# A gate made of pairs of nested tanh, with the first feed-forward tile reordered

## The chip, the cores and the metric

The kernel runs on one core of one Trainium2 chip. The core has five engines that each follow a list of their own: PE (TensorE, matmuls; PEld is its weight load), DVE (VectorE), ACT (ScalarE), POOL (GpSimd) and SP (SyncE, which here issues most DMAs). The metric is the device time of one execution in microseconds, as a median over runs; the profile is of one execution.

## The reference, cut to what matters

```python
# 4 x 8 heads of 768 x 64: attention in which only equal hash buckets see each other
x = attn_out.transpose(0, 2, 1, 3).reshape(3072, 512)
h = x @ w_in                                   # 3072 x 2048
sp = np.maximum(h, 0.0) + np.log1p(np.exp(-np.abs(h)))
g = h * erf(sp)                                # the gate
return (g @ w_out).astype(np.float32)          # 3072 x 512
```

## The kernel before

**Two parts.** Attention over 16 pairs of heads runs first, up to about 312 us. Then the feed-forward part takes the 3072 tokens in six tiles of 512 (t = 0 to 5). Both matrix products are done with seven block products in place of eight (Strassen in Winograd's form), so there are block sums around them, on DVE and POOL.

**Tile 0.** Its first product is done by one level: seven products P1 to P7 (`plain`), each in four chunks c = 0 to 3, 28 steps in all. A step accumulates into a PSUM bank named M1, M2, M4, M5, M6 or M7; `read_plain` copies a bank to one of four quarters of `h` on ACT, `complete` adds a bank to a quarter on DVE. A bank is free for the next step when it has been read. Chunks 0 and 1 make the first half (fl = 0) of each quarter, chunks 2 and 3 the second.

**Tiles 1 to 5.** Each of the seven products is done by seven smaller ones (`small`, Q1 to Q7). Their weight sums (`presum_inner`, called "inner") are made once by POOL while tile 0 runs, staged in a room, and written to DRAM by `keep_inner`, SP's transfers to `wi_P1` to `wi_P7`; `load_wi` brings them back into a ring that overlays `w_in`. POOL also makes the operand sums, `presum_x` (L347) and `presum_xi` (L1481).

**The gate.** Each quarter's half is a unit of 128 x 1024 numbers; six tiles have 48. `h * erf(softplus(h))` is computed as h times tanh of a product of factors. On ACT: `lead` (L1626, a sigmoid), `factor` (L1630, three sigmoids with scale and bias) and `saturate` (L1647, tanh). On DVE: `multiply` (L1636, one for each factor) and `gate` (L1651). Tiles `e` and `w` have two rooms each, so two units are in work at a time.

**The second product.** `presum_g` (L1696) sums gated quarters, `project` (L1725) multiplies them with `w_out` in seven products M1 to M7, interleaved on PE with the next tile's small products; `combine` (L1759 on DVE) adds and the result goes out. `presum_w` (L1443) makes the block sums of `w_out` on DVE: eight of them, into `wt`.

**The last pair of heads.** Its normalisation runs beside tile 0 (`late`): PE sums a divisor (`X`), ACT copies it, SP sends it through DRAM to be spread (`zd`, `zc`), DVE inverts it (L760, L763), SP spreads the inverse (`rd`, then `r`, which lands in `area`), DVE multiplies it in (`x_last`, L789), and SP writes the result. `late` 3 to 6 on DVE (L815) are the second halves of the weight sums P5, P6, P7 and P3. Tile 1's load of x waits for this chain.

**What sets the order.** Every operation is entered with an engine, a cost and a rank; `arrange` simulates the engines with these costs and picks, for each engine, the open operation that starts first, ties by rank. The result is a fixed list for each engine, which the hardware follows in order. Costs and ranks thus change only order.

Of the kernel before, what the change touches and what calls it, by code (L numbers as in the profile page):

```python
# [73 lines left out]
GATE_LEAD = float(np.exp(0.024672653620378578))  # L74
GATE_BIAS = 0.2070990400060388
GATE_S = tuple(
    (a, b, float(np.exp(d)))
    for a, b, d in (
        (1.0042202890675247, -2.7392697200635756, -1.6980318627393862),
        (0.9963684715182539, -0.22837759957137604, 0.7457328010609228),  # L80
        (1.6743181256578874, -5.977511012430903, 0.8413097454356667),
    )
# [106 lines left out]
def kernel(  # L189
# [45 lines left out]
    cq = const.tile([P, len(GATE_S) + 1], F32, name="cq")  # L235
# [56 lines left out]
    for j, c in enumerate([b for _, b, _ in GATE_S] + [GATE_BIAS]):  # L292
        nc.vector.memset(cq[:, j : j + 1], c)
# [936 lines left out]
    def feed_forward(pools, check, late):  # L1230
# [109 lines left out]
        def plain_ops():  # L1340
            for c in range(4):
                x, y, z = (("M1", "M2", "M4"), ("M5", "M6", "M7"))[c % 2]
                for k, (name, where, q, fn) in enumerate(
                    (
                        ("P1", x, 0, read_plain),
                        ("P2", y, 0, complete),
                        ("P6", x, 1, read_plain),
                        ("P5", z, 3, read_plain),
                        ("P7", x, 3, complete),
                        ("P3", z, 1, complete),  # L1350
                        ("P4", x, 2, read_plain),
                    )
                ):
                    fl = c // 2
                    pe(
                        "P",
                        (name, c),
                        1.73,
                        (0, (c + k / 7) / 4),
                        plain,  # L1360
                        (c, name, where, name in ("P1", "P2", "P5"), name in ("P4", "P2", "P3")),
                        reads=(xkey(0, name), ("w", name, fl)),
                        writes=(("bank", where),),
                    )
                    op(
                        (fn.__name__, c, q),
                        "ACT" if fn is read_plain else "DVE",
                        0.58 if fn is read_plain else 0.69,
                        (0, (c + k / 7) / 4),
                        fn,  # L1370
                        (c, q, where),
                        reads=(("bank", where),),
                        writes=part(0, q, fl),
                    )


        stage = [kept[f"h{n}"][:, :, :, :].rearrange("p l c t -> p (l c t)").rearrange("p (n c) -> p n c", n=4) for n in (4, 5)]

        def presum_inner(name, n, k):

            a = w_of(name)
            a11, a12 = a[:, 0, 0:WP], a[:, 1, 0:WP]
            a21, a22 = a[:, 0, WP:FH], a[:, 1, WP:FH]
            s1, s2, s3, s4 = (stage[n % 2][:, m, :] for m in range(4))
# [6 lines left out]
            nc.gpsimd.tensor_tensor(out=out_, in0=one_, in1=two_, op=op_)  # L1391

        def keep_inner(name, n):
            nc.sync.dma_start(out=wi_dram[name][:, 3:7, :], in_=stage[n % 2])
            if name in ("P6", "P7", "P5", "P3"):
                a = w_of(name)
                nc.sync.dma_start(out=wi_dram[name][:, 0:2, :], in_=a[:, 0:2, 0:WP])
                nc.sync.dma_start(out=wi_dram[name][:, 2, :], in_=a[:, 1, WP:FH])

        def inner_ops():  # L1400
            for n, name in enumerate(CHAIN):
                both = (("w", name, 0), ("w", name, 1))
                rooms = tuple(("h", 4 + n % 2, fl, tl) for fl in range(2) for tl in range(2))
                for k in range(4):
# [40 lines left out]
        def presum_w_ops():  # L1445
            for k in range(4):
                for fl in range(2):
# [3 lines left out]
                        1.25,  # L1451
                        (2, 0.2 + k / 10, fl),
                        presum_w,
                        (fl, k),
                        writes=(("wt", (3, 1, 2, 0)[k], fl),),
# [90 lines left out]
        def chain_ops(t):  # L1546
            for i, name in enumerate(CHAIN):
# [6 lines left out]
                    2.0,  # L1554
                    (1, t + (i - 1.2) / 7, 1),
# [67 lines left out]
        def lead(t, q, fl):  # L1623
            s = st["s", t, q, fl] = own("e")
            n = len(GATE_S)
            nc.scalar.activation(out=s, in_=unit(t, q, fl), func=AF.Sigmoid, bias=cq[:, n : n + 1])  # L1626

        def factor(t, q, fl, j):
            f = st["q", t, q, fl, j] = own("w")
            nc.scalar.activation(  # L1630
                out=f, in_=unit(t, q, fl), func=AF.Sigmoid, scale=GATE_S[j][0], bias=cq[:, j : j + 1]
            )

        def multiply(t, q, fl, j):
# [4 lines left out]
                scalar=GATE_S[j][2],  # L1639
# [12 lines left out]

        READY = {0: 3 / 7, 2: 5 / 7, 3: 6.3 / 7, 1: 1.0}

        def gate_ops(t, q):
            for fl in range(2):
                me = (t, q, fl)
                when = t + (READY[q] if t or again else (0.55, 1.0)[fl] + 0.03 * (0, 3, 1, 2)[q]) + 0.02 * fl
# [3 lines left out]
                    reads=mine, take=("e", me), table="sigmoid",  # L1662
                )
                previous = ("lead",) + me
                for j in range(len(GATE_S)):
                    key = ("w", (j, me))
                    op(
                        ("factor",) + me + (j,), "ACT", 1.14, (1, when, 1 + j), factor, me + (j,),
                        reads=mine, after=(("lead",) + me,), take=key, table="sigmoid",
                    )  # L1670
                    op(
                        ("multiply",) + me + (j,), "DVE", 1.22, (1, when, j), multiply, me + (j,),
                        after=(("factor",) + me + (j,), previous), free=(key,),
# [7 lines left out]
                    ("gate",) + me, "DVE", 1.22, (1, when, 5), gate, me,  # L1681
# [192 lines left out]
        def x_ops(t):  # L1874
# [6 lines left out]
            for k, (what, reads, into) in enumerate(  # L1881
# [10 lines left out]
                    1.2,  # L1892
                    (1, t - (0.5, 0.45, 0.3, 0.28)[k], 0),
# [11 lines left out]
        else:  # L1905
            if late:
                for k in range(3, 7):
# [3 lines left out]
                        ("late", k), "DVE", 1.2, (2, 0.1, k), late, (k,),  # L1911
                        reads=reads, writes=(("w", name, 1),), after=(("late", k - 1) if k > 3 else ("complete", 0, 1),),
# [154 lines left out]
```

## Time and profile before

| | us |
|---|---|
| median of 3 runs | 902.58 |
| lowest, highest | 902.26, 903.41 |
| the profiled execution, its own time | 902.08 |
| its span, first to last instruction | 899.9 |
| PE busy | 879.1 (98%) |
| DVE busy | 796.4 (88%) |
| ACT busy | 553.4 (61%) |
| POOL busy | 245.7 (27%) |

A duration in a row of the trace is of the profiled execution, whose time stands 2.2 us above its span and 0.5 us below the median. In rows of a timeline the columns are the start, the duration, the engine, the line, the operation, output and inputs, shape and count, and in brackets the idle time ahead with what ended it. A matmul of this kernel appears as two records.

### The profile page before, as it was taken

The page shows a single profiled execution, that of the slowest core. Times are in us where ns is not written, and L with a number is a line of the kernel's source. Part 1 is how long each engine was busy: PE and PEld are TensorE (multiplying, and loading weights), DVE is VectorE, ACT ScalarE, POOL GpSimd, SP SyncE. Part 2 cuts the span into 40 slices and gives each one's busy share as a digit, 9 for nine tenths or more (in the row PEclk, how much of TensorE's full clock was granted, in tenths as well). Part 3 has the DMA queues.
Part 4 walks back from the last instruction along what each step waited for, and adds up shares of the span by engine and source line. Part 5 has one row for each costly group of instructions (what it writes and reads, how often), then busy time and mean ns, then how long its engine had stood idle before and what let it go on. Part 6 is the DMA issues. An engine that isn't in the chain of part 4 may idle for free.

```text
span 899.9 us, 14621 instructions
## 1 busy us (share of the span) xinstructions
PE 879.1 (98%) x5728; PEld 669.9 (74%) x5728; DVE 796.4 (88%) x925; ACT 553.4 (61%) x759; POOL 245.7 (27%) x280
## 2 busy tenths in 40 slices
PE   9999999999999987799999999999999999999998
PEld 5445444444444566689999999999999999999986
DVE  6999999999998898999999979998899879987971
ACT  6888888788887626674458236814671458255720
POOL 1211111111110069893234313330423132210000
PEclk9999999999999999999999999999999999999999
DMA  9477765676652317745476336734574446543201
GB/s 232 133 203 203 213 173 156 189 189 185 169 142 61 110 75 284 268 162 198 161 205 233 129 129 188 247 119 161 161 229 161 165 127 201 176 156 119 56 12 39
DMA packets 96846, 146.60 MB, mean 163 GB/s; under 512 B 34830, under 2 KB 48190, under 8 KB 95872
## 3 DMA queue, kind: packets, MB, share of 16 engines
q1 hardware_dynamic: 88816, 122.01, 43.4%
q0 software_dynamic: 7504, 23.11, 9.4%
q8 instruction: 47, 0.77, 0.4%
q10 hardware_dynamic: 448, 0.46, 0.2%
q14 instruction: 31, 0.25, 0.1%
HBM read 113.21 MB, written 27.10 MB: 156 GB/s over the span
## 4 chain that ended last, share of the span: by engine, by line
PE 86%; DVE 10%; issue 3%; ACT 1%; DMA 0%; DVEq 0%; ACTq 0%
PE M L1725 30%; PE M L1499 23%; PE st L577 16%; PE av L662 13%; DVE e L1636 3%; PE bits L865 1%; PE bits L706 1%; DVE area L650 1%; DVE wt L1443 1%; DVE area L815 1%; PE M L1321 1%; DVE h L1338 1%; DVE h L1651 1%; ACT e_even L604 0%; PE warm L826 0%
## 5 line engine op out<-in xcount | busy, mean ns | idle before, releaser
L1636 DVE SCALAR_TENSOR_TENSOR e<-w,e 128x1024 f32<-128x1024 f32 x144 | 197.0, 1374 | 12.3 <-ACT w L1630 10.0
L1725 PE MATMUL M<-w_out_sb,h 128*128 128x256 f32 x752 | 185.1, 381 | 0.5 <-issue 0.5
L1630 ACT ACTIVATE w<-h,cq 128x1024 f32<-128x1024 f32 x144 | 159.6, 1141 | 17.0 <-DVE e L1636 16.4
L1522 DVE TENSOR_TENSOR h<-M,h 128x512 f32<-128x512 f32 x190 | 129.8, 684 | 29.4 <-PE M L1499 28.5
L577 PE MATMUL st<-q,k 64*128 64x384 f32 x768 | 155.1, 483 | 0.0
L1499 PEld LDWEIGHTS M<-area,w_in_sb 128*128 128x128 f32 x1120 | 145.3, 192 | 8.1 <-DVE h L1522 1.0
L1499 PE MATMUL M<-area,w_in_sb 128*128 128x128 f32 x1120 | 146.7, 275 | 0.3 <-DVE h L1522 0.3
L1725 PEld LDWEIGHTS M<-w_out_sb,h 128*128 128x128 f32 x752 | 133.6, 192 | 13.9 <-issue 0.8
L1626 ACT ACTIVATE e<-h,cq 128x1024 f32<-128x1024 f32 x48 | 54.8, 1142 | 133.5 <-DVE h L1522 110.9
L1499 PEld LDWEIGHTS M<-i,w_in_sb 128*128 128x128 f32 x840 | 108.9, 191 | 9.6 <-issue 3.2
L1499 PE MATMUL M<-i,w_in_sb 128*128 128x128 f32 x840 | 110.7, 275 | 2.1 <-ACT h L1519 1.1
L577 PEld LDWEIGHTS st<-q,k 64*128 64x128 f32 x768 | 68.5, 187 | 35.8 <-issue 34.4
L1725 PE MATMUL M<-wt,area 128*128 128x256 f32 x384 | 94.8, 380 | 0.0
L1647 ACT ACTIVATE e<-e 128x1024 f32<-128x1024 f32 x48 | 50.8, 1058 | 64.5 <-DVE e L1636 64.3
L650 DVE TENSOR_TENSOR area<-area 128x1536 f32<-128x1536 f32 (+1 forms) x46 | 79.2, 1721 | 6.5 <-ACT area L604 5.3
L1481 POOL TENSOR_TENSOR i<-area,i 128x128 f32<-128x128 f32 x70 | 45.9, 676 | 121.7 <-PE M L1499 120.5
L604 ACT ACTIVATE e_even<-st 128x768 f32<-128x768 f32 x96 | 73.9, 818 | 0.4 <-PE st L577 0.3
L604 ACT ACTIVATE area<-st 128x768 f32<-128x768 f32 x90 | 72.7, 810 | 0.3 <-PE st L577 0.3
L1725 PEld LDWEIGHTS M<-wt,area 128*128 128x128 f32 x384 | 67.6, 191 | 6.3
L1651 DVE TENSOR_TENSOR h<-h,e 128x1024 f32<-128x1024 f32 x48 | 63.2, 1317 | 2.9 <-ACT e L1647 2.9
L662 PE MATMUL av<-e_even,v 128*64 128x385 f32 x384 | 65.7, 490 | 0.0
L577 PE MATMUL st<-both 64*128 64x384 bf16 x384 | 63.0, 324 | 0.2 <-ACT e_even L604 0.2
(141 smaller groups left out, 1129.1 us busy)
## 6 DMA issues: line engine op xcount, KB each, us to landing
w_in_sb<-wi_P SPq DMA_DIRECT2D x35, 1792.0 KB, 8.1
raw<-in_w_out_dram POOLq DMA_DIRECT2D x16, 512.0 KB, 4.4
raw<-in_w_in_dram POOLq DMA_DIRECT2D x14, 512.0 KB, 6.1
wi_P<-h SPq DMA_DIRECT2D x7, 1024.0 KB, 4.0
v<-in_v_dram SPq DMA_DIRECT2D x32, 192.0 KB, 4.9
out_dram<-area SPq DMA_DIRECT2D x23, 256.0 KB, 5.8
q<-in_qkT_dram SPq DMA_DIRECT2D x30, 192.0 KB, 4.1
k<-in_qkT_dram SPq DMA_DIRECT2D x30, 192.0 KB, 4.2
```

The costliest lines, as they stand in the source:

```text
L577: nc.tensor.matmul(out=st[:, ab, 0:HS], lhsT=d["k" + src][rows, keys], rhs=d["q" + src][rows, cols], start=(part == 0), stop=(part == 1),)
L604: nc.scalar.activation(out=e[:, :, 0:HS], in_=st[:, :, 0:HS], func=AF.Exp, scale=scale)
L650: nc.vector.tensor_tensor(out=into, in0=one, in1=two, op=ALU.add)
L662: nc.tensor.matmul(out=d["av", half][rows, 0:w], lhsT=d["v"][:, g * GC + c, rows], rhs=e[:, ab, 0:w], start=(g == 0 and c == 0), stop=(g = ...
L1499: nc.tensor.matmul(out=out_[:, c, :], lhsT=ring[:, W_AT[q], n % 2, c * P : (c + 1) * P], rhs=x, start=(q in ("Q1", "Q2", "Q5") and c == 0) ...
L1522: nc.vector.tensor_tensor(out=out_, in0=bank_, in1=one, op=ALU.add)
L1626: nc.scalar.activation(out=s, in_=unit(t, q, fl), func=AF.Sigmoid, bias=cq[:, n : n + 1])
L1630: nc.scalar.activation(out=f, in_=unit(t, q, fl), func=AF.Sigmoid, scale=GATE_S[j][0], bias=cq[:, j : j + 1])
L1636: nc.vector.scalar_tensor_tensor(out=s, in0=st.pop(("q", t, q, fl, j)), scalar=GATE_S[j][2], in1=s, op0=ALU.add, op1=ALU.mult,)
L1647: nc.scalar.activation(out=s, in_=s, func=AF.Tanh, scale=GATE_LEAD)
L1651: nc.vector.tensor_tensor(out=h, in0=h, in1=st.pop(("s", t, q, fl)), op=ALU.mult)
L1725: nc.tensor.matmul(out=where[:, sub, :], lhsT=a[:, j // G, j % G, sub * P : (sub + 1) * P], rhs=b[:, j, :], start=first, stop=end, skip_gr ...
```

## The change

**The gate** has two factors in place of three. Each is now two nested activations, tanh(a2 * tanh(a1 * h + b1) + b2), both on ACT with the second in place; DVE multiplies once per pair. The lead stays a sigmoid.

```diff
-GATE_S = tuple(
-    (a, b, float(np.exp(d)))
-    for a, b, d in (
-        (1.0042202890675247, -2.7392697200635756, -1.6980318627393862),
...
+GATE_S = (
+    (((AF.Tanh, -0.182729044331454, -0.37562470687963295), (AF.Tanh, 4.998083443736455, 4.719439764051687)), -1.160741089374901),
+    (((AF.Tanh, -0.4999686770152115, 1.4869118698881234), (AF.Tanh, 1.7413382993796354, -3.01393763712213)), 0.7294259840089087),
 )
...
-        def factor(t, q, fl, j):
-            f = st["q", t, q, fl, j] = own("w")
+        def factor(t, q, fl, j, k):
+            f = unit(t, q, fl) if k == 0 else st["q", t, q, fl, j]
+            if k == 0:
+                st["q", t, q, fl, j] = own("w")
+            func, scale, _ = GATE_S[j][0][k]
...
-                out=f, in_=unit(t, q, fl), func=AF.Sigmoid, scale=GATE_S[j][0], bias=cq[:, j : j + 1]
+                out=st["q", t, q, fl, j], in_=f, func=func, scale=scale, bias=cq[:, column : column + 1]
```

**Tile 0's chunks** run in pairs, step by step, and a unit's lead now also waits by name for both of its chunks.

```diff
-            for c in range(4):
-                x, y, z = (("M1", "M2", "M4"), ("M5", "M6", "M7"))[c % 2]
-                for k, (name, where, q, fn) in enumerate(
+            for c0 in (0, 2):
+                for k, (name, n, q, fn) in enumerate(
...
+                    for c in (c0, c0 + 1):
+                        fl = c // 2
+                        where = (("M1", "M2", "M4"), ("M5", "M6", "M7"))[c % 2][n]
+                        rank = (0, (c0 + (2 * k + c % 2) / 7) / 4)
```

**The staging rooms** of the inner sums: `h4` and `h5` in turn for the first five products, and the first third of `wt` for P5 and P3.

```diff
+        ] + [wt[:, 0, :, :].rearrange("p f c -> p (f c)").rearrange("p (n c) -> p n c", n=4)]
+
+        def stage_of(n):
+            return n % 2 if n < 5 else 2
```

**The list**: other costs and ranks for `inner`, `presum_w`, `presum_xi`, `presum`, `late`, `multiply` and `gate`; for instance

```diff
-                        1.2,
-                        (1, 0.12 * n, k),
+                        1.8,
+                        (1, (0.1, 0.2, 0.3, 0.4, 0.5, 0.7, 0.9)[n], k),
```

What that does to the engines' lists begins where attention ends. PE, from the first plain step on (M1 to M7 are banks, X the divisor's bank; x4 are the four matmuls of a step), before and then after:

```order
L1321 MATMUL M1_3075<-area_76,w_in_sb_74 128x256 x4
L1321 MATMUL M2_3076<-area_76,w_in_sb_74 128x256 x4
L1321 MATMUL M1_3075<-area_76 128x256 x4
L1321 MATMUL M4_3077<-area_76 128x256 x4
L1321 MATMUL M1_3075<-area_76,w_in_sb_74 128x256 x4
L706 MATMUL X_3074<-area_76,ones_70 32x384 x4
L1321 MATMUL M4_3077<-area_76 128x256 x4
L1321 MATMUL M1_3075<-area_76,w_in_sb_74 128x256 x4
```
```order
L1317 MATMUL M1_3076<-area_76,w_in_sb_74 128x256 x4
L1317 MATMUL M5_3079<-area_76,w_in_sb_74 128x256 x4
L1317 MATMUL M2_3077<-area_76,w_in_sb_74 128x256 x4
L1317 MATMUL M6_3080<-area_76,w_in_sb_74 128x256 x4
L1317 MATMUL M1_3076<-area_76 128x256 x4
L1317 MATMUL M5_3079<-area_76 128x256 x4
L1317 MATMUL M4_3078<-area_76 128x256 x4
L702 MATMUL X_3075<-area_76,ones_70 32x384 x4
L1317 MATMUL M7_3081<-area_76 128x256 x4
L1317 MATMUL M1_3076<-area_76,w_in_sb_74 128x256 x4
```

Between two uses of bank M1 there was one other step; now there are three.

SP, around the last pair's divisor (`wi_P1`, `wi_P6`: the kept inner sums; `zd`, `zc`, `rd`: the divisor's way through DRAM), before and then after:

```order
L1394 DMA wi_P1_114<-h4_3086 128x2048
L746 DMA zd_3133<-area_76 4x384
L750 DMA zc_3134<-zd_3133 128x12
L768 DMA rd_3166<-zc_3134 128x12
L778 DMA area_76<-rd_3166 64x2x384 x2
L1394 DMA wi_P6_115<-h5_3087 128x2048
L1397 DMA wi_P6_115<-area_76 128x2x512
L1398 DMA wi_P6_115<-area_76 128x512
```
```order
L1399 DMA wi_P1_115<-h4_3087 128x2048
L742 DMA zd_3148<-area_76 4x384
L746 DMA zc_3149<-zd_3148 128x12
L1399 DMA wi_P6_116<-h5_3088 128x2048
L1402 DMA wi_P6_116<-area_76 128x2x512
L1403 DMA wi_P6_116<-area_76 128x512
L764 DMA rd_3196<-zc_3149 128x12
L774 DMA area_76<-rd_3196 64x2x384 x2
```

P6's three transfers moved ahead of the spreading of the inverse.

DVE, from the divisor's inverse on (M banks into `h` are `complete`; `x_last` is the last pair's normalisation), before and then after:

```order
L763 RECIPROCAL zc_3134<-zc_3134 128x12
L815 TENSOR_TENSOR area_76<-w_in_sb_74,area_76 128x2x512
L1338 TENSOR_TENSOR h0_3082<-M6_3079,h0_3082 128x512
L1976 TENSOR_REDUCE norms_122<-X_3074 1x32 x2
L1986 TENSOR_TENSOR norms_122<-norms_122 1x2x16
L1987 TENSOR_REDUCE top_123<-norms_122 1x1
L1988 TENSOR_SCALAR top_123<-top_123 1x1
L1996 TENSOR_SCALAR flag_121<-top_123 1x1
L1636 SCALAR_TENSOR_TENSOR e_3182<-w_3204,e_3182 128x1024
L1338 TENSOR_TENSOR h3_3085<-M5_3078,h3_3085 128x512
L789 SCALAR_TENSOR_TENSOR x_last_77<-x_last_77,ev_3026,area_76 128x384
```
```order
L759 RECIPROCAL zc_3149<-zc_3149 128x12
L1334 TENSOR_TENSOR h1_3084<-M4_3078,h1_3084 128x512
L1334 TENSOR_TENSOR h1_3084<-M7_3081,h1_3084 128x512
L785 SCALAR_TENSOR_TENSOR x_last_77<-x_last_77,ev_3027,area_76 128x384
L785 SCALAR_TENSOR_TENSOR area_76<-area_76,ev_3027 128x384
L1647 SCALAR_TENSOR_TENSOR e_3132<-w_3169,e_3132 128x1024
```

Nine rows, among them a weight sum and the first unit's first multiply, stood between the inverse and `x_last`; now two completions do, and the first unit's second multiply follows `x_last`.

More of the change, by code (lines that the diff above doesn't have):

```diff
@@ L234 @@
     tiny2 = const.tile([P, 1], F32, name="tiny2")
-    cq = const.tile([P, len(GATE_S) + 1], F32, name="cq")
+    cq = const.tile([P, 1 + sum(len(steps) for steps, _ in GATE_S)], F32, name="cq")
     w_in_sb = const.tile([P, NK, DFF], F32, name="w_in_sb")
@@ L1666, in gate_ops @@
                     key = ("w", (j, me))
-                    op(
[L1668 to L1673, printed above, removed]
+                    before = ("lead",) + me
+                    for k in range(len(GATE_S[j][0])):
+                        name = ("factor",) + me + (j, k)
+                        op(
+                            name, "ACT", 1.14, (1, when, 1 + j), factor, me + (j, k),
+                            reads=mine, after=(before,), take=None if k else key, table="sigmoid",
+                        )
+                        before = name
+                    op(
+                        ("multiply",) + me + (j,), "DVE", 1.3 if t else 1.6, (1, when, j), multiply, me + (j,),
+                        after=(before, previous), free=(key,),
                     )
```

111 lines of the change are left out of this document (60 added, 51 removed).

## The prediction, before the result

> **What bounds the kernel now.** I read first the busy time by stage, cut where the program changes: attention up to 312 us, the first feed-forward tile to 410, tiles 1 to 5 with their products interleaved to 843, the last products to the end. Columns: stage, its length, then busy us (and instructions) of PE, PEld, DVE, ACT and POOL, granted clock, DMA share, GB/s.
>
> ```profile
> 0.00:312.00 312.00, 310.80 (x2188) 151.56 (x2188) 282.87 (x391) 259.41 (x448) 45.17 (x82) 1.00 0.62 169
> 312.00:410.00 98.00, 82.73 (x397) 68.40 (x396) 94.23 (x75) 55.78 (x63) 82.36 (x51) 0.95 0.54 195
> 410.00:843.00 433.00, 432.67 (x2904) 403.97 (x2903) 388.23 (x430) 222.40 (x232) 118.12 (x148) 1.00 0.53 169
> 843.00:899.90 56.90, 52.94 (x245) 45.97 (x243) 31.03 (x32) 15.80 (x16) 0.00 (x0) 1.00 0.08 25
> ```
>
> PE is the bound everywhere but in the second row: from 410 to 843 it idles 0.33 us. Only from 312 to 410 does it lose time: 98 - 82.73 = 15.3 us idle, and 5% of clock on the 82.7 busy ones, 4.1 us. That is 19.4 us, and no rearrangement of vector and activation work can give more. There DVE is busy 94.2 of 98 us and POOL 82.4. Waits in that stage, and then PE's only one in the next (who waited for whom, total, times, longest):
>
> ```profile
> PE M L1321 <- ACT h L1334: 9.7, 6, 3.8
> PE M L1321 <- DVE h L1338: 3.5, 2, 2.1
> ...
> ACT w L1630 <- DVE e L1636: 8.2, 8, 1.9
> ...
> POOL h L1391 <- DMA wi_P<-h: 5.8, 2, 4.1
> ```
> ```profile
> PE M L1499 <- DVE h L1522: 0.3, 1, 0.3
> ```
>
> ```profile
> L1334 ACT COPY h<-M 128x512 f32<-128x512 f32 x16 | 9.1, 577 | 16.2 <-PE M L1321 11.4 <-DMA xs<-x 4.8
> ```
>
> Thirteen of the 15.3 us are the plain products of tile 0 (L1321) waiting for a bank to be copied out. The copying takes ACT 0.58 us; it is late because it stands in ACT's order behind activations that wait for DVE's multiplies (8.2 us of such waits). So DVE sets this stage. Its groups there, and the multiply's in the later tiles (count | busy us, mean ns | idle before):
>
> ```profile
> L1636 DVE SCALAR_TENSOR_TENSOR e<-w,e 128x1024 f32<-128x1024 f32 x22 | 39.6, 1807 | 2.7 <-ACT w L1630 2.1
> L1443 DVE TENSOR_TENSOR wt<-w_out_sb,wt 128x1024 f32<-128x1024 f32 x4 | 7.9, 2016 | 0.0
> ```
> ```profile
> L1636 DVE SCALAR_TENSOR_TENSOR e<-w,e 128x1024 f32<-128x1024 f32 x99 | 129.1, 1309 | 9.3 <-ACT w L1630 7.9
> ```
>
> **The factor that goes.** Each of 48 units loses one multiply and gains one activation: before 1 lead, 3 factors, 3 multiplies, 1 saturate, 1 gate; after 1 lead, 4 tanh, 2 multiplies, 1 saturate, 1 gate. In tiles 1 to 5 DVE loses 40 multiplies of 1.3 us; worth nothing, since PE idles 0.33 us there. In tile 0 it loses 8. At the stage's mean that is 8 x 1.807 = 14.5 us. But the same multiply takes 1.22 us when POOL is quiet, and POOL is slowed in the same stretch:
>
> ```profile
> 428.07 1.22 DVE L1636 SCALAR_TENSOR_TENSOR e<-w,e 128x1024 f32<-128x1024 f32 x1
> ```
> ```profile
> L1391 POOL TENSOR_TENSOR h<-area 128x512 f32<-128x512 f32 x6 | 13.5, 2251 | 0.0
> ```
> ```profile
> 340.58 1.27 POOL L1391 TENSOR_TENSOR h<-w_in_sb 128x512 f32<-128x512 f32 x1
> ```
>
> A POOL sum of 1.27 us takes 2.25 and a DVE multiply up to 2.25 when both are at work: they take turns. POOL's sums remain to be done, so taking a multiply out frees about its own 1.22 us: 8 x 1.22 = 9.8. The two ends are 9.8 and 14.5; I take 10. The Trainium skill ("SBUF — State Buffer", section "Who interferes with whom") has a rule for this: a DVE instruction with two SBUF inputs and a GpSimd instruction that reads SBUF hold a shared port in turn, and the second one waits out the first. The trace agrees (1.27 becomes 2.25); by that rule the term is 9.8, by the bare mean 14.5, and the forecast below would be lower by 4.7 us with the latter.
>
> **The activations added** are 48 x 1.14 us = 55 us of ACT, priced by the factors that are there (tanh with scale and bias bounded by them and by the saturate's 1.06 in the rows further down):
>
> ```profile
> L1630 ACT ACTIVATE w<-h,cq 128x1024 f32<-128x1024 f32 x99 | 109.1, 1139 | 3.1 <-DVE e L1636 2.8
> ```
>
> ACT is busy 222 of 433 us in tiles 1 to 5; 40 x 1.14 = 46 more make 62%. In tile 0 it goes from 55.8 to 65 of 98. The second tanh of a pair reads the first's result, which only lengthens a unit by about 0.1 us. Hidden by PE's unbroken work; without that cover, 1.2 us a unit. The place to check is the end, where tile 5's last four units face PE without interleaved work:
>
> ```profile
> 834.69 1.15 ACT L1626 ACTIVATE e<-h,cq 128x1024 f32<-128x1024 f32 x1 [0.71 <-DMA h<-area]
> ...
> 863.07 1.06 ACT L1647 ACTIVATE e<-e 128x1024 f32<-128x1024 f32 x1 [3.65 <-DVE e L1636]
> ```
> ```profile
> 866.67 1.22 DVE L1696 TENSOR_TENSOR area<-area,h 128x1024 f32<-128x1024 f32 x1
> ```
> ```profile
> 867.92 7.07 PE L1725 MATMUL M<-wt,area 128*128 128x256 f32 x32
> ```
>
> From 834.69 on, 24 activations and a copy need 24 x 1.14 + 0.58 = 28 us, to 862.6; today the last saturate starts at 863.07. Its sums end at 867.9, wanted for the second half of that product at 867.92 + 3.5 = 871.4. Zero, with 3.6 us of slack; 0 to 2 us in the range.
>
> **The chunks in pairs.** PE's list of 28 plain steps alternates two chunks, so a bank's copy has three other steps (a step is 8 matmul pieces, 1.8 us by the first row below) instead of one to hide in, and one only where the second pair begins. This answers PE's waits for ACT directly, but only as far as ACT's copies are not late for DVE's sake; it gives nothing beyond what DVE lets through. Also the unit of a first half is complete 5 steps, 9 us, sooner, which fills DVE's and ACT's early gap:
>
> ```profile
> 312.14 3.72 PE L1321 MATMUL M<-area,w_in_sb 128*128 128x256 f32 x16
> 318.18 5.31 PE L1321 MATMUL M<-area 128*128 128x256 f32 x16 [2.32 <-ACT h L1334]
> ...
> 340.57 2.50 PE L1321 MATMUL M<-area,w_in_sb 128*128 128x256 f32 x8 [3.81 <-ACT h L1334]
> ...
> 381.41 7.80 PE L1725 MATMUL M<-w_out_sb,h 128*128 128x256 f32 x32
> ```
>
> **The list and the rooms.** Of the eight weight sums (L1443) the last pair now waits for the staging room `wt` 0 and runs when PE is already unbroken: 2 x 2.0 us off DVE's stage, 2.4 by the take-turns reading; I take 3. POOL's sums of P5 and P3 go to that room instead of waiting for `h4`; the two POOL waits on that staging's DMA (5.8 us in the list of waits) go, to no direct effect.
>
> **What is added: SP's queue.** The three transfers that keep P6 now stand ahead of the last pair's `rd` and `r`. In the old list SP did this:
>
> ```profile
> 330.20 0.31 SPq L750 DMA_DIRECT2D zc<-zd  x1
> 336.16 0.32 SPq L768 DMA_DIRECT2D rd<-zc  x1
> 337.86 1.24 SPq L778 DMA_DIRECT2D area<-rd  x2
> 340.64 0.33 SPq L1394 DMA_DIRECT2D wi_P<-h  x1
> 341.01 0.43 SPq L1397 DMA_DIRECT2D wi_P<-area  x1
> 341.49 0.95 SPq L1398 DMA_DIRECT2D wi_P<-area  x1
> ```
> ```profile
> L789 DVEq EVENT_SEMAPHORE  x3: 21/21/21, 311.8 to 343.1; - x3
> ```
> ```profile
> 335.90 0.23 DVE L763 RECIPROCAL zc<-zc 128x12 f32<-128x12 f32 x1
> ...
> 344.80 1.61 DVE L789 SCALAR_TENSOR_TENSOR x_last<-x_last,ev,area 128x384 f32<-128x384 f32 x1
> 346.33 1.62 DVE L789 SCALAR_TENSOR_TENSOR area<-area,ev 128x384 f32<-128x384 f32 x1
> ```
> ```profile
> 323.50 2.25 POOL L1391 TENSOR_TENSOR h<-w_in_sb,h 128x512 f32<-128x512 f32 x1
> ```
> ```profile
> wi_P<-h SPq DMA_DIRECT2D x7, 1024.0 KB, 4.0
> ```
>
> `r` was there by 343.1, 5.2 us after its issue, and DVE came for it at 344.8. Now POOL must first end P6: P1's four sums end at 325.75, six more (two of P5, four of P6) at 2.0 to 2.25 end at 338 to 339. The three issues take 1.8, `rd` to `r` 1.7, the landing 5.2: 346.7 to 348, and up to 4.0 more (one 1 MB keep) if the small transfers wait behind the kept ones: 352. I take 349. DVE's new list ahead of it is three weight sums shorter (-6.0), with one multiply, one `late` and one completion more (+1.8, +2.2, +0.7): the reciprocal at about 335, two completions of 0.7, and DVE stands before `x_last` from about 337 or 338. So DVE stands some 11 us (9 to 15). Behind it on DVE is the second multiply of the first unit; ACT stands at that unit's saturate, behind which are the copies of chunk 2; PE has 18 steps until then, 18 x 1.8 and 0.9 for the divisor's sums from 312.1 on, to about 345, and then waits too. While DVE stands, POOL runs at 1.27 instead of 2.25, eight sums instead of five: about 1 us of turn saved on each of five, so 5 are paid back (0 to 5). Cost 6.
>
> **Sum, in span:** -10 - 3 + 6 = -7. Span 899.9 - 7 = 892.9; the profiled execution, 902.08, comes to 895.1; the median of 902.58 stands 0.5 above it: 895.6. I forecast 895.5.
>
> **Rivals.** *PE unbroken.* If `x_last` comes as early as DVE is ready, the cost of 6 falls away, and with multiplies at their mean the terms give 14.5 + 4 = 18.5, near the 19.4 at which PE is full: 884 to 889. For it: the pairs hide every copy. Against: the queue on SP.
>
> *Slower: the standing DVE.* If `rd` and `r` crawl behind the 1.75 MB of P6 and `x_last` starts after about 356 (337.5, plus 13 of gains, plus 5 paid back), the stand costs more than the factor gives; PE then cools as well: after the 2.32 us wait above, 16 pieces took 5.31 us where the first 16 took 3.72. At 361 it is 5 us slower plus 1.7 of clock: 909. Against: small transfers have not been seen to take over 5.2 us.
>
> *No difference: POOL's chain takes the wait.* Tile 1's first inner products need POOL's operand sums:
>
> ```profile
> 387.44 1.44 POOL L1481 TENSOR_TENSOR area<-area 128x128 f32<-128x128 f32 x1
> ```
> ```profile
> 397.25 2.02 PE L1499 MATMUL M<-i,w_in_sb 128*128 128x128 f32 x16 [1.07 <-ACT h L1519]
> ```
>
> They end at 393 and PE came at 397; PE now asks some 7 us of work sooner, since 12 instead of 28 matmuls with `w_out` (0.44 us each: 32 pieces in 7.07 above) stand ahead. In the new list P3's sums stand behind them (four of 2 us less), which pays for it; if POOL instead stands for tile 1's load, which hangs on `x_last`, PE gains only what is left: 901 to 904.
>
> **How the numbers follow.** Forecast's mechanism (loss of 3.5 to 13 us, 890 to 899) 0.55; PE unbroken 0.13; a gain worn down to 2 to 3.5 us 0.07; no difference 0.13; slower 0.12. What a measurement of this kernel can tell from no change is 0.2%, 1.8 us. Faster 0.75, same 0.13, slower 0.12. The range 886 to 904 leaves out slower and the lower half of the unbroken case, 0.19.
>
> **What would show it.** Right: DVE empty for 8 us or more before `x_last` (L785 after), SP's `rd` after P6's keep; the first product with `w_out_sb` near 374 instead of 381.41; 16 multiplies in tile 0; ACT over 60% in later tiles with PE still unbroken from 410; the end after 843 unchanged. Wrong: no stand at `x_last` (then nearer 887); PE waiting at L1507 for POOL or for the ring's loads; an idle PE before M6 at the end, which would mean ACT has become the bound there.

## The result, and the profile after

The changed kernel takes 889.7 us (median of 4 runs, 889.18 to 890.23), the kernel before beside it 902.4: a ratio of 0.9858, 95% interval 0.9841 to 0.9875. That is 12.7 us less where 7 were forecast. The profiled span is 888.4 us against 899.9, 11.5 less. The three later stages of the kernel after, in the columns of the first table of the prediction:

```profile
312.00:410.00 98.00, 88.97 (x489) 77.78 (x486) 77.46 (x77) 63.92 (x72) 72.14 (x56) 0.97 0.61 220
410.00:831.00 421.00, 420.47 (x2813) 393.48 (x2812) 343.03 (x384) 262.04 (x269) 111.47 (x142) 1.00 0.53 168
831.00:888.40 57.40, 53.44 (x249) 46.52 (x248) 27.91 (x29) 19.31 (x20) 0.00 (x0) 1.00 0.08 25
```

The last row is as long as before (57.4, was 56.9), the middle one is full. So the 11.5 us were won ahead of 410. What PE did up to there, by groups of instructions, before and then after (count | busy us, mean ns of one | idle ahead of them):

```profile
L1321 PE MATMUL M<-area,w_in_sb 128*128 128x256 f32 x128 | 31.2, 398 | 10.0 <-ACT h L1334 6.5 <-DVE h L1338 3.5
L1321 PE MATMUL M<-area 128*128 128x256 f32 x96 | 25.3, 418 | 3.3 <-ACT h L1334 3.3
L1725 PE MATMUL M<-w_out_sb,h 128*128 128x256 f32 x55 | 13.6, 395 | 0.0
L1499 PE MATMUL M<-area,w_in_sb 128*128 128x128 f32 x48 | 5.9, 277 | 0.0
L1499 PE MATMUL M<-i,w_in_sb 128*128 128x128 f32 x40 | 5.2, 281 | 2.0 <-ACT h L1519 1.1 <-DVE h L1522 0.9
```
```profile
L1317 PE MATMUL M<-area,w_in_sb 128*128 128x256 f32 x128 | 28.8, 381 | 0.3 <-ACT h L1330 0.3
L1317 PE MATMUL M<-area 128*128 128x256 f32 x96 | 23.6, 405 | 7.9 <-ACT h L1330 7.9
L1749 PE MATMUL M<-w_out_sb,h 128*128 128x256 f32 x64 | 15.6, 380 | 0.0
L1507 PE MATMUL M<-area,w_in_sb 128*128 128x128 f32 x96 | 12.1, 276 | 0.9 <-DMA w_in_sb<-wi_P 0.9
L1507 PE MATMUL M<-i,w_in_sb 128*128 128x128 f32 x71 | 9.2, 276 | 0.0
```

The same 224 pieces of plain product (the first two rows before, and the first two after) waited 13.3 us before and 8.2 after. The two rows count the seam between one group and the next twice, so their busy time is read for the line alone, before and then after:

```profile
312.00:410.00 98.00, 55.30 (x224) 44.49 (x224) 0.95 0.54 195
```
```profile
312.00:410.00 98.00, 51.30 (x224) 43.63 (x224) 0.97 0.61 220
```

In an unbroken stretch 16 pieces take 3.46 us (the starts 365.98 and 369.44 below), so 224 take 48.4: PE lost 6.9 us to running slow before, and 2.9 now. At 410 PE is ahead by 9 pieces with `w_out`, 0.22 us each at that rate, and by 79 small ones (16 in 1.95 us, below): about 11 us of work.

The stand before `x_last` came as forecast. DVE, ACT, PE and SP around it, from the timeline:

```profile
335.25 0.23 DVE L759 RECIPROCAL zc<-zc 128x12 f32<-128x12 f32 x1
...
347.90 1.43 DVE L785 SCALAR_TENSOR_TENSOR x_last<-x_last,ev,area 128x384 f32<-128x384 f32 x1 [11.27 <-DMA area<-rd]
...
349.77 1.21 DVE L1647 SCALAR_TENSOR_TENSOR e<-w,e 128x1024 f32<-128x1024 f32 x1
```
```profile
351.02 1.06 ACT L1658 ACTIVATE e<-e 128x1024 f32<-128x1024 f32 x1 [12.01 <-DVE e L1647]
...
353.02 0.56 ACT L1330 COPY h<-M 128x512 f32<-128x512 f32 x1
```
```profile
353.64 9.05 PE L1317 MATMUL M<-area 128*128 128x256 f32 x32 [7.88 <-ACT h L1330]
362.53 3.62 PE L1317 MATMUL M<-area,w_in_sb 128*128 128x256 f32 x16
365.98 3.62 PE L1317 MATMUL M<-area 128*128 128x256 f32 x16
369.44 3.62 PE L1317 MATMUL M<-area,w_in_sb 128*128 128x256 f32 x16
372.89 2.32 PE L1749 MATMUL M<-w_out_sb,h 128*128 128x256 f32 x10
```
```profile
380.98 1.95 PE L1507 MATMUL M<-i,w_in_sb 128*128 128x128 f32 x16
```
```profile
337.69 0.32 SPq L1399 DMA_DIRECT2D wi_P<-h  x1
...
339.53 1.26 SPq L764 DMA_DIRECT2D rd<-zc  x1
343.86 1.25 SPq L774 DMA_DIRECT2D area<-rd  x2
```

The chain reads from the bottom up: `rd` behind P6's keep, `r` 4.3 us later, DVE empty for 11.3 us, the first unit's saturate on ACT 12.0 us late, the copy behind it at 353.02, and PE empty for 7.9 us, its only long wait. The 32 pieces after it took 9.05 us where 32 unbroken take 7.17.

### The profile page after: what moved, and what is told of

It reads as the page before. It is cut to its first block, busy times and chain, and to the rows that moved or that the text cites. A ratio compares the mean times of both kernels' runs of the same rounds, so it can differ in the third digit from the quotient of the medians.

```text
span 888.4 us, 14568 instructions
## 1 busy us (share of the span) xinstructions
PE 873.7 (98%) x5728; PEld 670.0 (75%) x5728; DVE 730.9 (82%) x878; ACT 604.5 (68%) x807; POOL 228.7 (26%) x280
## 4 chain that ended last, share of the span: by engine, by line
PE 90%; DVE 5%; DMA 2%; ACT 1%; issue 1%; POOL 1%; SPq 0%; ACTq 0%; DVEq 0%; POOLq 0%
PE M L1749 32%; PE M L1507 24%; PE st L573 17%; PE av L658 13%; PE bits L861 1%; DMA w_in_sb<-wi_P 1%; PE bits L702 1%; DVE area L646 1%; DVE e L1647 1%; PE M L1317 1%; DVE area L811 1%; DVE wt L1450 1%; POOL h L1396 1%; PE warm L822 0%; ACT e_even L600 0%
## 5 line engine op out<-in xcount | busy, mean ns | idle before, releaser
L1507 PEld LDWEIGHTS M<-area,w_in_sb 128*128 128x128 f32 x1120 | 145.7, 192 | 8.2 <-ACT w L1641 1.3
L1507 PE MATMUL M<-area,w_in_sb 128*128 128x128 f32 x1120 | 146.7, 275 | 0.9 <-DMA w_in_sb<-wi_P 0.9
L1647 DVE SCALAR_TENSOR_TENSOR e<-w,e 128x1024 f32<-128x1024 f32 x96 | 129.2, 1346 | 20.4 <-ACT w L1641 20.2
L1749 PEld LDWEIGHTS M<-w_out_sb,h 128*128 128x128 f32 x752 | 132.8, 191 | 13.3 <-issue 0.8
L1641 ACT ACTIVATE w<-h,cq 128x1024 f32<-128x1024 f32 x96 | 109.2, 1137 | 9.4 <-DVE e L1647 9.4
L1507 PEld LDWEIGHTS M<-i,w_in_sb 128*128 128x128 f32 x840 | 109.2, 192 | 5.8 <-issue 0.5
L1641 ACT ACTIVATE w<-w,cq 128x1024 f32<-128x1024 f32 x96 | 110.2, 1148 | 2.0
L1507 PE MATMUL M<-i,w_in_sb 128*128 128x128 f32 x840 | 110.3, 275 | 0.0
L1489 POOL TENSOR_TENSOR i<-area,i 128x128 f32<-128x128 f32 x70 | 43.0, 634 | 120.0 <-PE M L1507 118.8
```

The source lines that it names most:

```text
L1507: nc.tensor.matmul(out=out_[:, c, :], lhsT=ring[:, W_AT[q], n % 2, c * P : (c + 1) * P], rhs=x, start=(q in ("Q1", "Q2", "Q5") and c == 0) ...
L1641: nc.scalar.activation(out=st["q", t, q, fl, j], in_=f, func=func, scale=scale, bias=cq[:, column : column + 1])
L1647: nc.vector.scalar_tensor_tensor(out=s, in0=st.pop(("q", t, q, fl, j)), scalar=GATE_S[j][1], in1=s, op0=ALU.add, op1=ALU.mult,)
L1749: nc.tensor.matmul(out=where[:, sub, :], lhsT=a[:, j // G, j % G, sub * P : (sub + 1) * P], rhs=b[:, j, :], start=first, stop=end, skip_gr ...
```

## The experiments

Nested gate, chunk order, rooms and list were taken apart first. Where no base is named, a ratio is to the kernel before, run on the same chip (902.0 to 902.9 us). The changed kernel was not run beside them, and the kernel before moved by 0.9 us from chip to chip, so a difference of about 1 us to the changed kernel is not read.

**1. The gate alone**, in the kernel before, with its old costs.

```diff
-GATE_S = tuple(
...
-        (1.6743181256578874, -5.977511012430903, 0.8413097454356667),
...
+GATE_S = (
+    (((AF.Tanh, -0.182729044331454, -0.37562470687963295), (AF.Tanh, 4.998083443736455, 4.719439764051687)), -1.160741089374901),
```

> Before with the new gate alone: nested tanh pairs, old chunk order, old rooms, old costs and ranks. Theory A (DVE's own work in tile 0 sets the stage): 8 multiplies fewer there free 10 us of DVE; part of it is lost since ACT's copies stand in line behind two more activations a unit: 894 to 898. Rival B (the longer ACT line makes PE's banks late, and the order matters more than DVE's sum): 900 to 906, PE waits for ACT copies longer than the 9.7 us of before. Rival C (the gate alone is the whole gain): 889 to 891.

894.2 us, ratio 0.9900 (0.9884 to 0.9917): theory A's size. PE's waits for copies of plain products fell from 9.7 to 5.0 us; the wait for ACT's copy at tile 1's small products grew from 1.1 to 5.0.

**2. The chunks in pairs alone**, with the old rooms, costs and ranks.

```diff
-            for c in range(4):
+            for c0 in (0, 2):
...
+                    for c in (c0, c0 + 1):
```

> Before with the chunks in pairs alone: old gate with three sigmoids, old rooms, old costs and ranks. Theory A (DVE sets the stage, pairs only move where PE waits): 899 to 903. Rival B (PE's waits came from the single step between two uses of a bank): the 13 us of waits go, 889 to 892.

916.1 us, ratio 1.0148 (1.0131 to 1.0165): slower by 13, and both theories missed. POOL, SP and PE show the wait that neither had:

```profile
396.48 2.24 POOL L1393 TENSOR_TENSOR h<-w_in_sb,h 128x512 f32<-128x512 f32 x1
```
```profile
398.74 0.32 SPq L1396 DMA_DIRECT2D wi_P<-h  x1
...
404.11 1.25 SPq L1470 DMA_DIRECT2D w_in_sb<-wi_P  x2
```
```profile
412.03 3.76 PE L1501 MATMUL M<-area,w_in_sb 128*128 128x128 f32 x16 [18.18 <-issue]
```

PE had ended its plain steps and all that was ready of the second product at 393.9. Tile 1's first weights overlay `w_in`, whose last inner sum POOL ended at 398.7; the load went out at 404.1 and PE stood 18.2 us. In the old list with pairs the sums of P7, which read `w_in`, come last but one on POOL, behind those of P4, P6 and P3. The pairs also bring a stand before `x_last` with them here (9.7 us) and one PE wait of 10.3 us for a copy behind it; PE's waits for copies sum to 11.4.

**3. The old gate in the changed kernel**: three sigmoids, with pairs, rooms and list as changed.

```diff
-GATE_LEAD = float(np.exp(4.14998867385302))
+GATE_LEAD = float(np.exp(0.024672653620378578))
...
+        (1.6743181256578874, -5.977511012430903, 0.8413097454356667),
```

> The changed kernel with the gate of before (three sigmoids, three multiplies), all else as changed. Theory A: DVE gets 8 x 1.2 to 1.8 us of work back in tile 0, so most of the gain of 12.7 us goes: 896 to 902. Rival B (order, pairs and rooms carry the gain): 889 to 892.

896.1 us, ratio 0.9927 (0.9911 to 0.9944), theory A. So pairs, rooms and list together give 6 to 7 of the 12.7 us, and the gate on top of them the rest (896.1 against 889.7). DVE still stands 10.8 us before `x_last` here.

**4. `rd` and `r` ahead of P6's keep** on SP, nothing else.

```diff
+        if late:
+            a, b = where(("keep", "P6")), where(("late", 1))
+            if a < b:
+                listed.insert(b, listed.pop(a))
```

> The changed kernel with one difference: on SP the spreading of the last pair's inverse (rd, r) stands ahead of the three transfers that keep P6; the lists of PE, DVE, ACT and POOL are the same. Theory A (SP's order makes DVE stand 11.3 us before x_last, and that makes PE stand 7.9 us): rd goes at 335.6 instead of 339.5, r at 337.4 instead of 343.9, x_last starts near 342.5 instead of 347.9, PE's wait falls from 7.9 to 2 to 3 us, time 883 to 886. Rival B (r's landing, not the queue ahead of it, is what is late, or another wait takes its place): x_last within 2 us of 347.9, or PE waits as long elsewhere: 888 to 890.

887.1 us, ratio 0.9830 (0.9813 to 0.9846): better than the changed kernel by 2.6 (its runs end at 887.4, those of the changed kernel begin at 889.2; the intervals of the two ratios just touch), less than expected. `r` came 6.6 us sooner and the stand fell to 5.0:

```profile
341.28 1.42 DVE L785 SCALAR_TENSOR_TENSOR x_last<-x_last,ev,area 128x384 f32<-128x384 f32 x1 [5.04 <-DMA area<-rd]
```

PE's wait for the copy fell from 7.9 to 3.7 and the first product with `w_out` came at 369.61 instead of 372.89: that order of transfers costs some 3 us.

**5. `x_last` behind the first unit's gate** on DVE, SP as changed.

```diff
+            a, b = where(("late", 2)), where(("gate", 0, 0, 0))
+            if a < b:
+                listed.insert(b, listed.pop(a))
```

> The changed kernel with one DVE step moved: the normalisation of the last pair's x (L785, twice) stands behind the first unit's second multiply and gate instead of ahead of them; SP's queue is as in the changed kernel, so rd still goes behind P6's keep and the r it waits for still lands near 348 us. Theory A (what the stand costs is the copies of chunk 2 on ACT, which stand behind the first unit's saturate, which waits for that multiply): ACT's wait of 12 us for e goes, PE's 7.9 us wait at the plain products and its lower clock behind it shrink below 3 us, first w_out product near 364 to 368 instead of 372.9, time 882 to 887 us. Theory B (the stand itself is lost DVE time and has to be made up): DVE still stands some 8 us before x_last, PE waits as long a little later, time 888 to 892.

888.9 us, ratio 0.9863 (0.9846 to 0.9879): 0.8 us under the changed kernel, with overlapping intervals, so no gain shown; B's range for the time. The stand fell to 5.0 us; PE's wait only to 4.8, since ACT now stands 9.2 us at a later factor (L1641), whose room is freed by a multiply behind `x_last`.

**6. Both moves.** The two edits above together.

> The changed kernel with both moves: rd and r ahead of P6's keep on SP, and x_last behind the first unit's gate on DVE. Theory A: r lands near 341, when DVE has the second multiply and the gate behind it, so no stand is left; PE stands under 2 us between 312 and 400 and the time is 879 to 884 us, 3 to 8 below the kernel with the swap alone (887.1). Theory B (PE's end is bound by something behind the first tile once DVE is relieved, the tile 1 operand sums or its load): 885 to 888, with a new PE wait at the small products of tile 1 between 375 and 410.

890.1 us, ratio 0.9865 (0.9849 to 0.9882): no stand is left on DVE, PE ends its plain steps 7.6 us sooner than in the changed kernel (365.27), and the time is that of the changed kernel. Theory A is refuted as to the time; B's mechanism is there, and its price higher than B had it. POOL, SP and PE:

```profile
363.39 2.25 POOL L1396 TENSOR_TENSOR h<-w_in_sb,h 128x512 f32<-128x512 f32 x1
```
```profile
366.11 0.56 SPq L1476 DMA_DIRECT2D w_in_sb<-wi_P  x1
```
```profile
376.14 3.75 PE L1507 MATMUL M<-area,w_in_sb 128*128 128x128 f32 x16 [6.39 <-issue]
```

The load that tile 1 needs goes out at 366.1, after POOL's last sum of P4 (in the changed kernel at 368.2), and PE's first small product starts at 376.14 (there 378.25). PE comes 7.6 us sooner and the load 2.1, so PE stands 6.4 us there; the 16 pieces behind the wait take 3.75 us where unbroken ones take 1.95. The profile names no releaser for this wait ("issue"); that it is the load is read from the times here, and tested in run 9.

**7. The old chunk order in the changed kernel.**

```diff
-            for c0 in (0, 2):
+            for c in range(4):
```

> The changed kernel with the 28 plain steps in the order of the kernel before (chunk by chunk), all else as changed. Theory A (the pairs keep PE fed by giving each bank's copy three steps to hide in): PE waits again for ACT's copies in many places between 312 and 345 (6 us there in the kernel before, 0.3 in the changed one), time 893 to 900. Theory B (what keeps PE fed is only that DVE is relieved by the multiplies, as 894 of the gate alone with the old list suggests): 888 to 892. Rival C (the pairs bring the trouble at x_last, since ACT's first unit comes sooner): below 888.

892.6 us, ratio 0.9884 (0.9863 to 0.9906): the pairs are worth some 3 us, between A and B, and the intervals of the two kernels overlap. One early wait returns, of 2.3 us, and not the many of theory A: PE in the first 18 us of tile 0, here and then in the changed kernel:

```profile
312.00:330.00 18.00, 15.68 (x70) 12.21 (x67) 15.79 (x13) 2.94 (x6) 12.04 (x7) 0.91 0.26 104
```
```profile
312.00:330.00 18.00, 18.00 (x90) 14.57 (x87) 17.74 (x15) 9.09 (x13) 11.62 (x6) 1.00 0.26 104
```

Part of it is paid back: DVE has more to do ahead of `x_last`, which starts at 345.36, and stands 2.6 us there instead of 11.3.

**8. The old rooms in the changed kernel.**

```diff
-            return n % 2 if n < 5 else 2
+            return n % 2
```

> The changed kernel with P5 and P3 staged in the old room h4/h5 instead of in the free half of wt. Theory A (without the third room POOL's sums for P5 and P3 wait for the landing of earlier keeps, run later and beside DVE at 2.25 us, and tile 1's operand sums and loads come late, as in the kernel with pairs alone, where PE stood 18 us at the small products of tile 1): POOL's last inner sum ends after 396 us, PE stands 3 to 12 us at the small products between 375 and 420, time 893 to 902. Theory B (the rooms only move waits that POOL has time for): 889 to 891.

899.2 us, ratio 0.9960 (0.9948 to 0.9972): the third room is worth 9.5 us (7 to 10, since the seven runs lie between 896.5 and 900.1), in A's range, yet not by A's wait. PE's waits from 312 to 420:

```profile
PE M L1749 <- DVE h L1662: 7.5, 3, 3.5
PE M L1317 <- ACT h L1330: 4.9, 2, 4.6
```

Without the room POOL's list has P5's sums later, and P3's ahead of tile 1's third operand sums instead of behind them: these start at 391.52, in the changed kernel at 381.23. The last weight sum ends at 391.5, sooner than in the changed kernel (394.3), so A's sign did not come. In PE's list most of the products with `w_out` that the changed kernel spreads between small ones stand in one piece ahead of the second group of these; PE waits there for DVE's gates, where the changed kernel has no such wait.

**9. P5's sums on POOL behind tile 1's first operand sums**, on top of both moves.

```diff
+            for name in [("inner", "P5", k) for k in range(4)] + [("keep", "P5")]:
+                a, b = where(name), where(("presum", 2, 0)) - 1
+                if a < b:
+                    listed.insert(b, listed.pop(a))
```

> The kernel with both moves (rd and r ahead of P6's keep, x_last behind the first gate; 890.1 us), and POOL's four sums for P5 with their keep moved from their places among the sums of P6, P2 and P7 to behind tile 1's third operand sums (presum_xi 1, 2). There PE stood 6.4 us at the first small product, waiting for tile 1's first weight load, which was issued at 366.1, after POOL's last sum of P4 at 365.6. Theory A (that load hangs on the length of POOL's chain up to P4's sums, and P5's three sums of 1.6 to 2.25 us in it are what is late): P4's sums end near 360, the load is issued near 361, PE's 6.4 us wait falls below 1.5, time 881 to 885 us. Theory B (DVE and POOL share their port, so whatever is moved the two together end no earlier, or the load's issue hangs on something else, such as P4's room or PE's last plain product in that half): the load stays after 364, PE waits 4 to 6 us, time 887 to 890.

886.1 us, ratio 0.9824 (0.9808 to 0.9840), the best of all here, between the ranges of A and B: 3.6 us under the changed kernel and 4.0 under kernel 6.

```profile
359.89 2.26 POOL L1396 TENSOR_TENSOR h<-w_in_sb,h 128x512 f32<-128x512 f32 x1
```
```profile
362.61 0.56 SPq L1476 DMA_DIRECT2D w_in_sb<-wi_P  x1
```
```profile
372.09 3.75 PE L1507 MATMUL M<-area,w_in_sb 128*128 128x128 f32 x16 [5.01 <-issue]
```

P4's last sum ends 3.5 us sooner, the load goes out 3.5 us sooner and PE's small product starts 4.05 us sooner. So theory A's link is shown: the load hangs on POOL's chain, and in kernels 6 and 9 PE's time does too. Its size was too hopeful: PE came 2.7 us sooner as well, and still stands 5.0.

**10. The kernel before without its third sigmoid.**

```diff
-        (1.6743181256578874, -5.977511012430903, 0.8413097454356667),
```

> The kernel before with the third sigmoid factor left out of the gate: 48 multiplies and 48 activations fewer, nothing else moved (part of the computation is left out). Beside the nested gate alone (894.2 us), which drops the same 48 multiplies and adds 48 activations, it prices the 96 activations between them. Theory A (DVE sets the first tile's pace and the activations lie beside it): 892 to 896. Theory B (ACT's copies of the plain products stand behind the activations, 16 of them of 1.14 us in the first tile): 884 to 890.

899.4 us, ratio 0.9969 (0.9959 to 0.9979): 2.9 us, and both theories missed from above. The same 8 multiplies left tile 0 as in kernel 1, which gained 8.7 with more work on ACT. Tile 0 itself did gain: PE's first small product of tile 1 starts 6.0 us sooner than in the kernel before (383.10, was 389.05). It is lost again behind it. PE in kernel 10 (its profiled execution took 901.2 us):

```profile
383.10 1.95 PE L1498 MATMUL M<-area,w_in_sb 128*128 128x128 f32 x16
...
394.03 3.76 PE L1498 MATMUL M<-i,w_in_sb 128*128 128x128 f32 x16 [3.80 <-ACT h L1518]
```

PE waits 3.8 us there, where the kernel before waits 1.1, runs slow after it, and waits 2.5 us more behind 410 (before 0.8). DVE's timeline in tile 0, kernel 10 and then kernel 1 (`h<-M,h` is `complete`):

```profile
354.68 0.68 DVE L1337 TENSOR_TENSOR h<-M,h 128x512 f32<-128x512 f32 x1
355.28 6.11 DVE L1635 SCALAR_TENSOR_TENSOR e<-w,e 128x1024 f32<-128x1024 f32 x3
361.31 0.68 DVE L1337 TENSOR_TENSOR h<-M,h 128x512 f32<-128x512 f32 x1
```
```profile
347.51 0.68 DVE L1334 TENSOR_TENSOR h<-M,h 128x512 f32<-128x512 f32 x1
348.12 1.70 DVE L1635 SCALAR_TENSOR_TENSOR e<-w,e 128x1024 f32<-128x1024 f32 x1
350.83 0.69 DVE L1334 TENSOR_TENSOR h<-M,h 128x512 f32<-128x512 f32 x1 [1.01 <-PE M L1317]
```

With short factors the planner packs two multiplies and a gate, or three multiplies, between two completions, and DVE stays full (92.7 of 98 us, before 94.2). With nested ones a unit waits longer for its factors, and one multiply, at times with a gate, stands between completions; DVE is then even early for PE's banks. In kernel 1 DVE is busy 80.9 of the 98 us.

**11. The changed kernel with the inner tanh left out of both factors.**

```diff
-    (((AF.Tanh, -0.182729044331454, -0.37562470687963295), (AF.Tanh, 4.998083443736455, 4.719439764051687)), -1.160741089374901),
+    (((AF.Tanh, 4.998083443736455, 4.719439764051687),), -1.160741089374901),
...
-    (((AF.Tanh, -0.4999686770152115, 1.4869118698881234), (AF.Tanh, 1.7413382993796354, -3.01393763712213)), 0.7294259840089087),
+    (((AF.Tanh, 1.7413382993796354, -3.01393763712213),), 0.7294259840089087),
```

> The changed kernel with the inner tanh left out of both factors (part of the computation is left out): 96 activations fewer, the multiplies, the list and the rooms as changed, except where the planner orders differently without them. Theory A (the activations are hidden; the stand at x_last sets the first tile): 887 to 891, the changed kernel's 889.7 give or take the list. Theory B (ACT's longer work in the first tile or at the end is on the path): 880 to 886.

891.3 us, ratio 0.9874 (0.9858 to 0.9891): 109 us of ACT fewer and no gain, just above A's range, within the uncertainty of the changed kernel. The stand is the same (11.0 us). The planner orders anew here too, so only the sum of both effects is read: zero.

**12. Kernel 1 with the inner tanh planned but not issued**, so that the other engines keep kernel 1's order.

```diff
         def factor(t, q, fl, j, k):
-            f = unit(t, q, fl) if k == 0 else st["q", t, q, fl, j]
             if k == 0:
-                st["q", t, q, fl, j] = own("w")
+                st["q", t, q, fl, j] = own("w"); return
+            f = unit(t, q, fl)
```

> The kernel with the nested gate alone (old list and chunks; 894.2 us), with the inner tanh of both factors planned as before but not issued (part of the computation is left out). In the first tile DVE, PE, POOL and SP keep the order of that kernel; ACT issues 16 activations of 1.14 us fewer there, 96 in all. Leaving out the third sigmoid alone, with the planner free, gave only 3 us (899.4); its list puts two or three multiplies between two completions of plain products (h<-M,h), that of the nested gate one. Theory A (the list makes the difference, the activations cost nothing): 892.5 to 895. Theory B (the longer chain on ACT itself spaces the multiplies out and lets the completions through): 897 to 900. Theory C (the activations are on the path of the first tile and a better list hides that): below 891.

892.1 us, ratio 0.9890 (0.9873 to 0.9906), 0.4 below A's range; beside kernel 1 (0.9900) the intervals overlap, so 0 to 2 us for the activations. A unit of this kernel has the same number of instructions as one of kernel 10, on DVE and on ACT; only the order of the lists (and the function on ACT) differs, and kernel 12 is 7.3 us faster. So most of what the gate gains comes from the order that the planner writes for it. Which place in the lists does it is not shown: at tile 1's first small product kernel 12 is 3.3 us ahead of kernel 10 (379.85, where that had 383.10), so a little under half of it is won in tile 0; for the rest, PE waits 2.8 us instead of 3.8 at the next small products and 0.6 instead of 2.5 behind 410.

## Why the prediction was right, and where its sum was off

**The number.** 889.7 lies 0.3 us below the 890 to 899 of the forecast's own mechanism and 0.7 above the 884 to 889 of its rival *PE unbroken*. That it lies in the whole range of 886 to 904 is owed to the width of the range, and so in part to luck: most terms of the sum were too small a gain or too high a cost, as the following shows.

**What bounds the kernel.** Right as to the place: all of the gain lies ahead of 410, in PE's waits for banks and the slow running behind them. PE is also idle for 4.0 us in the last row, which the prediction passed over; that is the same after. The ceiling of 19.4 us was too low. It took 4.1 us for slow running from the mean granted clock; the plain steps' own durations show 6.9, and the first 32 pieces with `w_out` 0.7 more (7.80 us, where 32 take 7.07 in the row at 867.92 of the prediction).

**The step that failed: the sum counts DVE and waiting only.** It had no term for PE's clock. PE's idle time from 312 to 410 went from 15.3 to 9.0 us, 6.2 less, and that is close to the 7 forecast; the plain steps' slow running fell by another 4.0 us, and that of the first pieces with `w_out` by 0.7. Where the remaining 0.6 of the 11.5 us lie stays open. The prediction used slow running only in its ceiling (4.1 us) and in the slower rival (1.7). By places: the second product began at 372.89 (forecast 374, was 381.41), and from there to the end it took 515.5 us where it took 518.5; of these 3.0, 1.1 are PE's waits up to 410 (0.9, was 2.0).

**The factor, 10 us.** The size came out near: the gate alone gave 8.7, and with half of its tanh not issued 9.9. The reason given covers only a part. The prediction said that DVE sets the stage, so that a multiply less frees its own 1.22 us. Kernel 10 has the 8 multiplies fewer; tile 0 gained 6.0 us by its profile, and the kernel 2.9. With the same number of instructions, kernel 12's order gained 9.9. So what the multiplies free is kept or lost by the order that the planner writes around it. What they are worth in the old order, held fixed, no run shows.

**The activations, zero.** Right within 2 us (runs 11 and 12; in run 11 the order could change too), and ACT is busy 262 of 421 us, 62%, with PE still full.

**The pairs, nothing beyond what DVE lets through.** Wrong in the old list, where they cost 13 us for POOL's chain. With the changed list they keep PE unbroken from 312 to 345 and seem worth some 3 us, which the intervals of run 7 do not establish. Together with the list they brought the first unit's lead 17.5 us sooner (321.40, was 338.90), where the prediction counted 9.

**The list and the rooms, 3 us.** Far too small: with only the third room taken away, 9.5 us are lost (run 8). The prediction saw two POOL waits go "to no direct effect"; the room also decides what the planner can put between PE's products with `w_out`.

**SP's queue, a cost of 6.** The stand was forecast at 11 us (9 to 15), with `x_last` at 349: 11.3, at 347.9. Its net price was too high: with `rd` first the time falls by 2.6 us, and with no stand at all (run 6) by nothing. What is late next explains that: tile 1's first load, behind POOL's chain. While DVE stood, POOL's sums ran faster; the last of eleven in a row at 1.26 to 1.28 us, from the changed kernel's timeline:

```profile
347.65 1.26 POOL L1396 TENSOR_TENSOR h<-w_in_sb,h 128x512 f32<-128x512 f32 x1
```

With DVE at work the same sum takes 2.25 (run 6, at 363.39). The Trainium skill ("SBUF — State Buffer", section "Who interferes with whom") says that such instructions of DVE and GpSimd share a port and that the one waits out the other; the traces agree, 1.26 against 2.25. So a microsecond of DVE's stand is in part POOL's gain.

**The rivals.** *PE unbroken* had the time nearly right (884 to 889, measured 889.7) by another way: the stand was there. Its condition, no stand, came true in run 6 and did not give that time. *POOL's chain takes the wait* named POOL's operand sums or tile 1's load of x; what came late in runs 2, 6 and 9 was the first weight load, behind POOL's weight sums, so the chain was right and its last link another. In the changed kernel it is 0.9 us, the wait at L1507 above. *The standing DVE* on the slower side did not come: `x_last` started 8 us ahead of the 356 from which it decides.

**The marks named ahead** came: DVE empty over 8 us, `rd` behind P6's keep, the first product with `w_out` near 374, ACT over 60%, the end unchanged. Of the marks of being wrong, one came in small: PE waiting at L1507 for the ring's load, 0.9 us.

## What to carry to other kernels

Price a wait of PE with what follows it: here 15.3 us of waiting ahead of 410 came with 7.6 of slow running before, and 9.0 with 2.9 after, and the durations of like instructions show that better than a mean clock. Where a planner writes the order, an instruction removed or lengthened moves all the others; to know what the instruction itself costs, hold the order fixed and leave only it out, as run 12 does for the inner tanh and no run here for the multiply. Before a stand is removed, look for what is late next and what the stand lets run: here the load behind POOL's chain already held PE by 0.9 us.

## What the runs showed of the hardware that was not expected

After 6.4 us of waiting, 16 small matmul pieces took 3.75 us instead of 1.95, and after 7.9 us 32 plain ones 9.05 instead of 7.17: the price in these pieces was near 1.9 us in both, and no more after the 18.2 us of run 2 (3.76). It does not grow with the wait: in run 5, 16 plain pieces took 6.57 us instead of 3.62 after a wait of only 4.8. After 2.3 us of waiting 16 plain pieces took 5.31 us in the kernel before and 3.72 in run 10, so there it is sometimes nothing. A 6 KB transfer to DRAM behind 1.75 MB on the same queue let its follower go 4.3 us after its own issue, where it took 1.7 without them (run 4). Loads of 1792 KB took 7.8 us from issue to landing in the median of the profile; the first one of tile 1 went out at 368.22 in the changed kernel and held PE until 378.25, 10.0 us, with another transfer issued 1.4 us behind it. In runs 6 and 9, where the profile does not name what PE waited for, it was 10.0 and 9.5.
